# Score matmuls of seven head groups on 64 by 32 array tiles instead of 64 by 64, in a fused attention and two-layer network kernel

## The chip, the cores and the metric

The kernel runs on one core of one Trainium2 chip. The metric is device time of one execution in microseconds (us). The core's engines are TensorE (PE, with its weight loads shown as PEld), VectorE (DVE), ScalarE (ACT), GpSimd (POOL) and SyncE (SP); they run at the same time, each in the order of its own program, and wait for one another through semaphores.

## The reference

Attention with normalised queries and keys, then a two-layer network with a leaky activation. 8 batches, 12 heads, 448 positions, head size 64; the network takes 3584 rows of 768 to 2048 and back.

```python
def rmsnorm(x, g):
    return x / np.sqrt(np.mean(x * x, axis=-1, keepdims=True) + 1e-06) * g
q_n, k_n = rmsnorm(q, g_q), rmsnorm(k, g_k)
scores = np.matmul(q_n, k_n.transpose(0, 1, 3, 2)) / np.sqrt(64)
attn = np.exp(scores - np.max(scores, axis=-1, keepdims=True))
attn = attn / (np.sum(attn, axis=-1, keepdims=True) + 1e-09)
x = np.matmul(attn, v)           # then (batch * position, head * 64)
h = x @ w_in
out = (np.maximum(h, 0.0) + alpha * np.minimum(h, 0.0)) @ w_out
```

## The kernel before

**Tiling.** The twelve heads of a batch are split into two halves g, and a *group* y is two heads of each half: three groups a batch, 24 in all (y = 0 to 23). Each group's queries and keys are squared, summed, scaled and transposed so that the head size lies on the partitions. The 448 keys are cut into J = 7 pieces j of 64. A *score tile* (y, j) holds the scores of one piece of keys against all 448 queries for the four heads: a PSUM tile `sc` of 128 partitions by two banks. Partitions 0 to 63 are half g = 0 and 64 to 127 are g = 1; the two banks are the two heads `par` of each half. There are two such PSUM tiles, used in turn.

**The scores.** `score(y, j)` (L355 to L370) makes one tile. The contraction is over the head size, 64, so a matmul takes 64 rows of the array, and `par` chooses which half of the rows. Its output columns are keys: with m = 64 one matmul gives all 64 keys of a head, four matmuls a tile, each on an array tile of 64 rows by 64 columns (64*64 in the profile). With m = 32 the keys are cut in two (`c`), eight matmuls a tile on array tiles of 64 by 32. Each matmul streams 448 columns and is preceded by its own weight load (the piece of `kT`). L358 chooses m: 64 for y < EARLY, which is 3 * G = 9, else 32. `soft` (L372, ACT at L376) takes the exponential of a whole tile into `expT`.

**Denominators and values.** `den` and `den_pre` sum `expT` over the keys with matrices of ones, `attv` multiplies it with the values. Both use array tiles of 64 by 32 in all groups: `over_keys` (L380, matmuls at L387) and `ones_over` (L411), 56 matmuls a set; PSUM tiles `dn`, `dnb`, `av`, `avb`. Denominators go through ACT (logarithm and exponential, `rden`), and DVE multiplies values by them into `xT`, the input of the network.

**The network.** `up` (matmuls at L501, tiles `hT`, `hTa`, `hTb`) multiplies by `w_in`, ACT and DVE form the activation `gT`, and `down` (L563, `op`, `opa`) and, later, the products of `quad_a`, `quad_b` and `quad_c` (L628, `qx`, `qz`, `qc`) multiply by `w_out`. These matmuls use the whole array, 128 by 128. The transposes of queries and keys (`tps`) do too.

**Order.** The order of all engines' work is written out by hand. The main loop runs over *bursts* n: each has two to four score tiles with their exponentials, in some bursts a set of denominators or values between the tiles, and then a stretch of network work. So TensorE goes from 128 by 128 to the scores' shape, in some bursts to the 64 by 32 of denominators or values and back, and again to 128 by 128. Up to about 34 us there is no network work yet. The first seven groups (y < 7) are transposed on TensorE, the rest by DMA.

**Queues.** Inputs come through SP's queue (and a little ACT's), weights and values through POOL's. The last part of the weights `w_in` and `w_out` lands at 77.5 us, beside the inputs of the next groups.

Of the kernel before, what the change touches and what calls it, by code (L numbers as in the profile page):

```python
# [21 lines left out]
def kernel(  # L22
# [28 lines left out]
    EARLY = 3 * G  # L51
# [303 lines left out]
    def score(y, j):  # L355
        qT, kT = qkT[y, "q"], qkT[y, "k"]
        sc = pss.tile([128, 2, 512], FP32, name="sc", tag="sc")
        m = 64 if y < EARLY else 32  # L358
        for c in range(64 // m):
            for par in range(2):  # L360
                for g in range(2):
                    nc.tensor.matmul(  # L362
                        out=sc[ds(64 * g + m * c, m), par, :S].rearrange(
                            "p (j c) -> p j c", j=J
                        ),
                        lhsT=kT[ds(64 * par, 64), j, g, ts(c, m)],
                        rhs=qT[ds(64 * par, 64), :, g, :],
                        start=True,
                        stop=True,
                    )  # L370
        scs[y, j] = sc
# [409 lines left out]
    m = 0  # L781
    while m < NG * J or steps:
# [21 lines left out]
        while len(bursts[n]) < limit and m < NG * J:  # L804
            y, j = divmod(m, J)
# [244 lines left out]
    for n in range(NB):  # L1050
# [6 lines left out]
        for t in first_tiles:  # L1057
            if t == (0, J - 2):
                spin(1)
            elif t == (1, J - 3):  # L1060
                spin(2, False)
            elif t == (1, J - 2):
                spin(1, False)
            elif t == (0, J - 1):
                turn_one(1, "q")
            elif t == (1, 0):
                turn_one(1, "k")
            elif t == (1, J - 1):
                turn(2)
            score(*t)  # L1070
            if n == den_at[G - 1] - 1 and t == tiles[-1]:
                begin(0)
                begin(1)
            elif lead and t == tiles[0]:
                soft(*t)
                den(dens[n])
                attv(avs[n], 0, True, (log, invert))
            elif lead and t == tiles[1]:
                begin(2)
# [30 lines left out]
        for t in () if lead else tiles[len(first_tiles) : 3]:  # L1110
            score(*t)
            soft(*t)
        if n in avs and len(avs[n]) == 2 and avs[n] != (0, 1):
            attv(avs[n], 1)
        for t in () if lead else tiles[max(len(first_tiles), 3) :]:
            score(*t)
            soft(*t)
# [3 lines left out]
        if n in roots:  # L1121
            y = roots[n]
# [112 lines left out]
```

## Time and profile before

| | us |
|---|---|
| median of 3 runs (413.71 to 420.57) | 417.81 |
| the profiled execution | 417.34 |
| its span, first to last instruction | 415.6 |
| TensorE busy | 398.9 |
| ACT busy | 273.4 |
| DVE busy | 265.8 |
| POOL busy | 255.2 |
| score matmuls 64 by 64, 252 of them, busy | 21.9 |
| score matmuls 64 by 32, 840 of them, busy | 31.8 |

The granted TensorE clock was 0.994 of full speed on average. Matmuls overlap, so that the busy time of a group is the time in which at least one of it ran; a matmul of 448 columns is shown with about 350 ns, while such matmuls follow one another every 189 ns on the whole array. Score tiles of the first nine groups run from 11.4 to 120.6 us, those from group 2 on from 26.7 us.

"issue" as the end of an idle time means that the profile shows nothing that the engine waited for. Instructions are brought to the engines by DMA too; queue 8 of the DMA table is of the kind "instruction".

### The profile page before, as it was taken

What the parts mean: (1) busy time and instruction counts of PE and PEld (TensorE: products, weight loads), DVE (VectorE), ACT (ScalarE), POOL (GpSimd) and SP (SyncE); (2) the same over time, 40 slices, a digit from 0 to 9 for tenths busy, and PEclk for the clock granted to TensorE, in tenths of its full rate; (3) what the DMA queues carried; (4) which work ended last, traced back from release to release, by engine and by line L of the source; (5) the groups of instructions that cost most, each with busy time, mean ns of one, the idle gap of its engine ahead of it and who ended that gap; (6) DMA issues with size and microseconds to landing.
All of it is one profiled execution on the core that took longest, in us unless ns stands there. A gap on an engine that the chain in (4) does not pass through costs nothing. (4 is left out here: it accounts for less than half of the span.)

```text
span 415.6 us, 11768 instructions
## 1 busy us (share of the span) xinstructions
PE 398.9 (96%) x5055; PEld 208.3 (50%) x5055; DVE 265.8 (64%) x421; ACT 273.4 (66%) x390; POOL 255.2 (61%) x180
## 2 busy tenths in 40 slices
PE   6889899999999999989999999999999999999996
PEld 3344345544455445544455445444555445655564
DVE  3876675575556485795788585958577755465322
ACT  4798697778956785666786897884667884135110
POOL 5589695779596974887094857476633507400870
PEclk9899999999999999999999999999999999999999
DMA  8999999976827596829957596279412800320133
GB/s 182 238 234 229 162 210 168 231 193 88 178 36 177 136 125 112 182 64 175 141 81 175 130 211 139 67 167 193 95 41 48 141 4 21 77 58 0 38 95 96
DMA packets 68019, 53.39 MB, mean 128 GB/s; under 512 B 35568, under 2 KB 67456, under 8 KB 67968
## 3 DMA queue, kind: packets, MB, share of 16 engines
q1 hardware_dynamic: 53520, 39.54, 45.5%
q0 software_dynamic: 13472, 11.81, 20.0%
q10 hardware_dynamic: 976, 1.31, 1.3%
q8 instruction: 39, 0.64, 0.7%
q14 instruction: 12, 0.10, 0.1%
HBM read 45.62 MB, written 11.01 MB: 136 GB/s over the span
## 5 line engine op out<-in xcount | busy, mean ns | idle before, releaser
L376 ACT ACTIVATE expT<-sc,expb 128x896 f16<-128x896 f32 x168 | 162.2, 1003 | 45.9 <-PE sc L362 45.7
L501 PE MATMUL hT<-xT,w_in_sb 128*128 128x448 f16 x546 | 113.7, 353 | 2.1 <-issue 1.7
L501 PEld LDWEIGHTS <-w_in_sb 128*128 128x128 f16 x768 | 72.7, 98 | 76.6 <-issue 12.3
L545 DVE TENSOR_TENSOR gT<-hT,gT 128x448 f16<-128x448 f32 x91 | 56.6, 623 | 40.3 <-ACT gT L541 39.2
L210 POOL TENSOR_TENSOR qs<-nat,rr 128x896 f16<-128x896 f32 x36 | 60.5, 1702 | 34.7 <-issue 21.8
L182 POOL TENSOR_TENSOR sq<-nat 128x896 f32<-128x896 f32 x32 | 53.5, 1683 | 41.8 <-DMA nat<-in_q_dram 29.6
L541 ACT ACTIVATE gT<-hT,cols 128x448 f16<-128x448 f32 x90 | 56.9, 633 | 30.0 <-PE hT L501 29.7
L362 PE MATMUL sc<-qT,kT 64*32 64x448 f16 (+1 forms) x1092 | 53.7, 358 | 4.3 <-ACT expT L376 2.0
L628 PEld LDWEIGHTS <-gT 128*128 128x128 f16 x352 | 33.5, 98 | 26.8 <-issue 5.7
L501 PE MATMUL hTa<-xT,w_in_sb 128*128 128x448 f16 x210 | 45.4, 353 | 0.0
L190 DVE TENSOR_REDUCE ss<-sq 128x14 f32<-128x896 f32 (+1 forms) x37 | 38.5, 1052 | 0.9 <-POOL sq L182 0.8
L486 DVE TENSOR_TENSOR xT<-av,rden 64x448 f16<-64x448 f32 (+1 forms) x37 | 27.2, 734 | 14.2 <-PE av L387 8.9
L545 DVE TENSOR_TENSOR gT<-hTa,gT 128x448 f16<-128x448 f32 x35 | 21.8, 623 | 19.5 <-ACT gT L541 19.2
L541 ACT ACTIVATE gT<-hTa,cols 128x448 f16<-128x448 f32 x35 | 22.2, 635 | 18.2 <-PE hTa L501 18.1
L362 PEld LDWEIGHTS <-kT 64*32 64x32 f16 (+1 forms) x1092 | 16.0, 93 | 36.0 <-issue 29.9
L563 PE MATMUL op<-w_out_sb,gT 128*128 128x384 f16 x160 | 27.4, 326 | 0.0
L387 PEld LDWEIGHTS <-vt 64*32 64x32 f16 x1344 | 19.9, 92 | 12.4 <-issue 2.8
L616 POOL TENSOR_TENSOR gs<-gT 128x1024 f16<-128x1024 f16 x3 | 6.4, 2125 | 30.4 <-DVE gT L545 28.1
L563 PEld LDWEIGHTS <-gT 128*128 128x128 f16 x192 | 18.0, 98 | 13.4 <-issue 2.3
L387 PE MATMUL av<-expT,vt 64*32 64x448 f16 x896 | 24.3, 350 | 0.3 <-DVE osb L676 0.3
L624 POOL TENSOR_TENSOR gT<-gT 128x1024 f16<-128x1024 f16 x11 | 23.4, 2128 | 0.0
L628 PE MATMUL qx<-w_out_sb,gT 128*128 128x384 f16 x120 | 20.8, 326 | 1.2 <-DVE rden L430 1.2
(149 smaller groups left out, 494.0 us busy)
## 6 DMA issues: line engine op xcount, KB each, us to landing
out_dram<-osb SPq DMA_DIRECT2D x107, 96.0 KB, 3.0
nat<-in_q_dram SPq DMA_DIRECT2D x40, 224.0 KB, 4.2
nat<-in_k_dram SPq DMA_DIRECT2D x40, 224.0 KB, 5.1
vt<-in_v_dram POOLq DMA_DIRECT2D x16, 336.0 KB, 8.0
w_in_sb<-in_moe_w_in_dram POOLq DMA_DIRECT2D x12, 256.0 KB, 7.8
w_out_sb<-in_moe_w_out_dram POOLq DMA_DIRECT2D x4, 768.0 KB, 9.7
arena<-in_q_dram SPq DMA_DIRECT2D x6, 224.0 KB, 7.4
arena<-in_k_dram SPq DMA_DIRECT2D x6, 224.0 KB, 6.8
```

The source lines that it names most:

```text
L182: nc.gpsimd.tensor_mul(out=sqf[:, c], in0=src[:, c], in1=src[:, c])
L190: nc.vector.tensor_reduce(out=o[:, c], in_=sqs[y, nm][:, c], axis=AXIS_X, op=ALU.add)
L210: eng.tensor_mul(out=t.rearrange("p j h d -> p h j d"), in0=nat[y, nm], in1=rr_t[y][:, "qk".index(nm)].unsqueeze(3).broadcast_to((128, 2, ...
L362: nc.tensor.matmul(out=sc[ds(64 * g + m * c, m), par, :S].rearrange("p (j c) -> p j c", j=J), lhsT=kT[ds(64 * par, 64), j, g, ts(c, m)], r ...
L376: nc.scalar.activation(out=expT[y][:, j], in_=scs[y, j][:, :, :S], func=AF.Exp, scale=QK_SCALE, bias=expb[:, 0:1],)
L387: nc.tensor.matmul(out=accs[g][ds(32 * n, 32), :S], lhsT=weights(g, y, par, c, j), rhs=expT[y][ds(64 * g, 64), j, par, :], start=(j == 0), ...
L486: nc.vector.tensor_mul(out=x, in0=av, in1=r)
L501: nc.tensor.matmul(out=hT[:, :S], lhsT=w_in_sb[:, g * G + i, ts(ft, 128)], rhs=xT[b][:, g, i, :], start=(i == 0 and g == 0), stop=(i == G ...
L541: nc.scalar.activation(out=g, in_=hT[:, :S], func=AF.Copy, scale=alpha_sb[:, ft : ft + 1])
L545: nc.vector.tensor_max(out=g, in0=hT[:, :S], in1=g)
L563: nc.tensor.matmul(out=op[:, :OH], lhsT=gT[:, ft, ts(tile % J, 128)], rhs=w_out_sb[:, ft, ts(oh, OH)], start=(ft == 0), stop=(ft == NF - 1),)
L628: nc.tensor.matmul(out=bank[:, c], lhsT=g[:, ft], rhs=v[:, ft, c], start=(first and ft == 0), stop=(ft == HF - 1), skip_group_check=True,)
```

## The change

One line of `score`: the bound below which m is 64 goes from EARLY (9) to 2. Groups 0 and 1 keep array tiles of 64 by 64; groups 2 to 8, the third to the ninth, get 64 by 32, as groups 9 to 23 have. A tile of theirs is then eight matmuls with eight weight loads instead of four with four; outputs, inputs and everything else stay.

```diff
     def score(y, j):
         qT, kT = qkT[y, "q"], qkT[y, "k"]
         sc = pss.tile([128, 2, 512], FP32, name="sc", tag="sc")
-        m = 64 if y < EARLY else 32
+        m = 64 if y < 2 else 32
         for c in range(64 // m):
             for par in range(2):
                 for g in range(2):
```

## The prediction

> **What bounds the kernel now.** I read the page first: busy shares, the slices, then the chain that ended last.
>
> ```profile
> PE 398.9 (96%) x5055; PEld 208.3 (50%) x5055; DVE 265.8 (64%) x421; ACT 273.4 (66%) x390; POOL 255.2 (61%) x180
> ...
> PE 29%; DVE 1%; ACT 0%; issue 0%; DVEq 0%
> ...
> q8 instruction: 39, 0.64, 0.7%
> ```
>
> TensorE is busy 96% of the span, and the chain back from the end hardly leaves it. So from about 43 us on, TensorE time saved or lost arrives at the end nearly one for one. The third row matters later: TensorE's 10,110 instructions are far the most of any engine, and 39 instruction packets of 16.4 KB are 256 instructions each if they are TensorE's (39 x 256 = 9,984).
>
> Next, TensorE's timeline (start, length, instruction, count) in a burst of 64x64 scores (first line group) and in a late burst that is already 64x32:
>
> ```profile
> 68.67 0.57 PE L362 MATMUL sc<-qT,kT 64*64 64x448 f16 x8
> 69.17 1.52 PE L387 MATMUL dn<-expT,ones 64*32 64x448 f16 x56
> 70.62 0.38 PE L362 MATMUL sc<-qT,kT 64*64 64x448 f16 x4
> 70.93 2.77 PE L563 MATMUL op<-w_out_sb,gT 128*128 128x384 f16 x16
> ```
> ```profile
> 157.21 0.57 PE L362 MATMUL sc<-qT,kT 64*32 64x448 f16 x16
> 157.60 1.51 PE L387 MATMUL dn<-expT,ones 64*32 64x448 f16 x56
> 158.92 0.37 PE L362 MATMUL sc<-qT,kT 64*32 64x448 f16 x8
> 159.23 2.77 PE L563 MATMUL op<-w_out_sb,gT 128*128 128x384 f16 x16
> ```
>
> The same work, three score tiles and one set of denominators, takes 70.93 - 68.67 = 2.26 us with two changes of array shape inside it and 159.23 - 157.21 = 2.02 us with none: 0.12 us a change. Twice the matmuls cost nothing themselves: eight 64x32 ones run together as four 64x64 ones do (two tiles alone between 128x128 work take 89.87 to 90.38 = 0.51 us as 64x64, and 0.50 us late in the kernel as 64x32).
>
> Last, the one long idle time of TensorE between 30 and 170 us, and the windows around it (window, length, TensorE busy and count, weight loads, DVE, ACT, POOL, granted clock, DMA share, GB/s):
>
> ```profile
> 39.92 1.69 PE L501 MATMUL hTb<-xT,w_in_sb 128*128 128x448 f16 x8
> 43.33 0.92 PE L501 MATMUL hT<-xT,w_in_sb 128*128 128x448 f16 x4 [1.72 <-issue]
> ```
> ```profile
> 36.52:43.32 6.80, 5.09 (x128) 2.56 (x128) 1.47 (x2) 3.77 (x4) 6.55 (x7) 1.00 1.15 219
> 68.60:92.50 23.90, 23.75 (x417) 11.97 (x417) 13.53 (x20) 17.77 (x24) 14.98 (x10) 1.00 0.99 211
> 92.50:122.00 29.50, 29.32 (x342) 14.38 (x340) 16.01 (x25) 23.35 (x34) 24.30 (x17) 1.00 0.57 98
> ```
>
> The values' last input, xT, is written by DVE until 41.45, yet TensorE starts at 43.33, released by nothing that the profile shows. At 36.28 a score tile is also torn: its first matmul starts at 36.28, the other three from 36.52. Between the two restarts lie 128 matmuls and 128 weight loads, exactly 256 instructions: one packet of the instruction queue. The packets fit (the DMA view, narrowed until one instruction packet fills it): one runs from 33.76 to 34.94 and TensorE goes on at 36.52; the next from 40.87 to 41.80, and it goes on at 43.33, some 1.55 us behind the packet each time. So TensorE here runs out of instructions, and one block is on its way while one is worked off. From entering a block (36.52) to having the next (43.33) took 6.80 us while the DMA engines were full (share 1.15). At 70 to 77 us the next close call: entry between 69.6 and 70.6, packet until 75.44, the block's first instruction at 76.69, with the queue just empty: 6.1 to 7.1 us, and nothing lost. Above 110 us, with the share at 0.57, packets start 0.2 to 3 us after the entry, and I count no such stall.
>
> **The change part by part.** It touches the scores of groups 2 to 8, 49 tiles.
>
> *Removed: changes of shape.* Only bursts with denominators or values have them. By the timeline after 60 us, from the first score to the next other work, against the late twin: 68.67 burst 0.24 (two changes); 73.64 to 77.67, two sets of values, 4.03 against 3.53 (165.83 to 169.36) = 0.50; 80.37, whose denominators wait 0.15 us for DVE anyway, only the way back, 0.10; 84.90 0.24; 110.47, which waits 0.18 us, 0.12; 118.28 to 121.88, 3.60 against 3.23 = 0.37. Sum 1.57 us, all on the path. The changes before 42 us are not counted: what is gained there ends in the wait for the instruction packet. The bursts with scores alone: 0.
>
> *Added: instructions.* 49 tiles x 4 matmuls, each with its weight load, = 392, one and a half blocks. Their run time is nothing (above); their fetch is the unknown of this change, bounded by 0 (packets early enough, as above 110 us) and 8.0 us a block (from 28.5, the earliest entry before the 36.52 restart). I take 6.8, the one row where both ends are seen, in the same stretch. Each block now ends earlier in the program, by 8 instructions for each changed tile before it.
>
> *The first stretch, by that price.* The block that ended at 36.52 has seven changed tiles ahead and ends 56 instructions earlier, in the transposes of group 3 (the eleventh of fourteen, at 33.4 on the old clock). Its predecessor is entered some 0.4 us sooner (16 instructions, and two changes of shape saved), so the packet serves at 36.1. TensorE stands from 33.4 to 36.1. Then: three transposes 0.15, score tile (2,5), tile (2,6) and the eight hT matmuls to 38.4, tile (3,0) to 38.7. The denominators of group 2 need (2,6) through ACT, two exponentials of 0.9 us a step behind (2,5)'s scores at 36.9: 38.8. They start at 39.0 instead of 36.84. The following block (64 instructions earlier, two thirds through the values at 38.17) is wanted at 41.1 and comes at 36.1 + 6.8 = 42.9. Then the rest of the values 0.45, tile (3,1) 0.6, eight hTb 1.5: the hT matmuls of 43.33 start at 45.5. Meanwhile xT is ready at 44.7. Loss 2.2 us, in place of the old stall and not on top of it. With packets as prompt as later this would be 0; at 8.0 us a block 3.6.
>
> *The second stretch.* Between 53 and 73 us a block lasts 8 us and more: no wait. The block that is entered at the scores of 73.64 ends with the tile at 77.35, less 0.61 us of saved changes, 76.7. The sequencer reaches it early: the 16 matmuls ahead are 32 instructions, and earlier packets (81.6 to 85.64, 92.7 to 96.28) start 4 us behind the instruction 64 places before the entry, which is here 70.6. With 6.1 to 7.1 us behind that: 76.7 to 77.7. I take 0.4 us; if the sequencer isn't ahead, it is 73.4 + 6.8 = 80.2, a loss of 3.5. The next block, 7.2 us long, is covered. Above 92 us the ends only move; the shortest stretch from the place 64 ahead of an entry to the block's end is 6.2 us where it was 5.9: 0.
>
> *Sum:* -1.57 + 2.2 + 0.4 = +1.0 us. The profiled execution took 417.34 us (span 415.6, 1.7 around it), so 418.4; the median of the runs shown is 0.5 above it, so **418.9 us**.
>
> [...]
>
> **The rivals.**
> - *The packets come in time; only changes of shape remain.* For it: above 110 us none is late, and DMA traffic is not the same in every execution. Against: shares of 1.15 and 0.99 in the two stretches, two late packets in this trace. It decides from a fetch below about 5 us. Median 417.8 - 1.6 = 416.2, still within 2%.
> - *The lateness adds up.* At 8.0 us a block the first stretch costs 3.6; a sequencer not ahead at 73.4 gives a block at 81.4, 4.7, and 0.8 at the next, which is 7.2 long. The standing engine may lose its clock: after a 3.4 us window with 1.07 us busy (7.9 to 11.3) the granted clock was 0.50 for the next one; the window 31.8 to 35.2 would keep about 1.5 busy, and half a clock there costs up to 1.7. Sum 3.6 + 4.7 + 0.8 + 1.7 - 1.6 = +9.2: 427. Against: every term at its worst.
> - *Little of anything:* half of the early loss is taken up by ACT's and DVE's slack: -1.57 + 1.1 + 0.2, about 417.5. This is inside the forecast's own range.
>
> **How the numbers follow.** Forecast (with the last rival) 0.52, its own range 416.5 to 421.5; packets in time 0.23; adding up 0.25, of which some 0.20 pass the bound. 2% (8.4 us) is about what a measurement of this kernel can tell from no change; its three runs spread from 413.7 to 420.6. Faster by more would need five times the saving that I find: 0.04. Slower 0.20, within 0.76. Range for 8 in 10: from 414.9 (the first rival, less a little spread) to 426 (most of the second).
>
> **What would show it.** Right: the scores at 68.67 to the op matmuls take 2.0 us; a TensorE idle time released by "issue" among the transposes near 33.4 and one inside the values of group 2, 256 instructions apart, each 1.5 us behind an instruction packet; the first hT after xT at about 45.5; hT and op matmuls of the same lengths as before. Wrong: no such idle times (first rival), several near 77 to 86 us or a granted clock of 0.5 near 35 us (second), or a difference that starts after 122 us, where I put nothing.

## The result and the profile after

The changed kernel took 419.06 us (median of 13 runs, 417.48 to 421.14), the kernel before 417.26 us over 13 runs. The ratio is 1.0077, 95% interval 1.0051 to 1.0103: 2.1 to 4.3 us slower, 3.2 in the middle. The ratio goes by the fast runs of each kernel and is no quotient of the two medians, which lie 1.8 us apart. A second set of six runs, on the same chip as two other kernels, gave 1.0112 (1.0066 to 1.0158). The profiled execution took 418.89 us, its span is 417.1.

Page of the changed kernel, the rows that were shown of the one before:

```profile
PE 397.3 (95%) x5251; PEld 209.6 (50%) x5251; DVE 267.7 (64%) x421; ACT 273.3 (66%) x390; POOL 256.1 (61%) x180
...
PE 29%; DVE 1%; ACT 0%; issue 0%; DVEq 0%
...
q8 instruction: 41, 0.67, 0.7%
```

196 matmuls and 196 weight loads more, two instruction packets more, and TensorE is busy for 1.6 us less while the span is 1.5 us longer. The time went into standing.

The timeline of TensorE in the changed kernel (start, length, instruction, count, idle time ahead of it) shows where:

```profile
31.59 0.79 PE L335 MATMUL tps<-ident,arena 128*128 128x128 f16 x11
34.19 0.34 PE L335 MATMUL tps<-ident,arena 128*128 128x128 f16 x3 [1.81 <-issue]
...
38.11 1.12 PE L387 MATMUL av<-expT,vt 64*32 64x448 f16 x37
42.03 0.74 PE L387 MATMUL av<-expT,vt 64*32 64x448 f16 x19 [2.79 <-issue]
...
44.42 0.92 PE L501 MATMUL hT<-xT,w_in_sb 128*128 128x448 f16 x4
```

The row of fourteen transposes is torn after eleven, the values of group 2 after 37 of 56, and nothing in the profile releases TensorE from either pause. The old pause ahead of the hT matmuls is gone: they now follow the hTb matmuls at once. The windows view of the changed kernel (window, length, TensorE busy and count, weight loads, DVE, ACT, POOL, granted clock, DMA share, GB/s) counts what lies between the two restarts:

```profile
34.19:42.02 7.83, 5.04 (x128) 2.41 (x128) 2.67 (x3) 4.78 (x5) 7.61 (x9) 1.00 1.16 230
```

Again 128 matmuls and 128 loads: one block of 256 instructions, whose successor took 7.8 us to come.

Setting the same matmuls of both profiles side by side, counted in the program, gives the course of the difference (start in the changed kernel less start in the one before, us):

| matmul | before at | difference |
|---|---|---|
| denominators at 27.54 | 27.54 | -1.41 |
| first hT after xT | 43.33 | +1.09 |
| denominators of group 3 and 4 | 69.17 | +0.97 |
| avb | 75.90 | +0.50 |
| opa, behind the tile at 77.35 | 77.67 | +0.99 |
| opa | 122.19 | +0.24 |
| hT | 137.12 | +1.75 |
| qx | 179.50 | +1.17 |
| from 284 to the end | | +1.55 |

Of the -1.41, 1.28 us stand before the first changed instruction (the score at 26.72 of the kernel before); the rest is its first change of shape. In the profile of before the granted clock was 0.50 from 11.3 to 14.7 us, in that of after it was 1.00 up to the last microseconds. So this pair of profiles hides some 1.3 us of the loss: 1.5 + 1.3 = 2.8 us, within the 2.1 to 4.3 of the ratio.

Second stretch, TensorE's timeline of the changed kernel:

```profile
69.76 0.57 PE L362 MATMUL sc<-qT,kT 64*32 64x448 f16 x16
70.14 1.51 PE L387 MATMUL dn<-expT,ones 64*32 64x448 f16 x56
71.47 0.37 PE L362 MATMUL sc<-qT,kT 64*32 64x448 f16 x8
71.78 2.77 PE L563 MATMUL op<-w_out_sb,gT 128*128 128x384 f16 x16
...
77.72 0.35 PE L362 MATMUL sc<-qT,kT 64*32 64x448 f16 x1
78.34 0.38 PE L362 MATMUL sc<-qT,kT 64*32 64x448 f16 x7 [0.27 <-issue]
```

The burst that took 2.26 us takes 71.78 - 69.76 = 2.02 us, as its late twin does. The tile that stood at 77.35 is torn after its first matmul: the third block that comes late.

### The profile page after: what moved, and what is told of

The parts are those of the page before. It is cut to its first block, busy times and chain, and to the rows that moved or that the text cites. A ratio compares the mean times of both kernels' runs of the same rounds, so it can differ in the third digit from the quotient of the medians.

```text
span 417.1 us, 12160 instructions
## 1 busy us (share of the span) xinstructions
PE 397.3 (95%) x5251; PEld 209.6 (50%) x5251; DVE 267.7 (64%) x421; ACT 273.3 (66%) x390; POOL 256.1 (61%) x180
## 5 line engine op out<-in xcount | busy, mean ns | idle before, releaser
L210 POOL TENSOR_TENSOR qs<-nat,rr 128x896 f16<-128x896 f32 x36 | 61.5, 1727 | 42.2 <-issue 23.7
L387 PEld LDWEIGHTS <-vt 64*32 64x32 f16 x1344 | 21.0, 93 | 14.4 <-issue 4.8
```

Of the source, the lines that this page charges most:

```text
L210: eng.tensor_mul(out=t.rearrange("p j h d -> p h j d"), in0=nat[y, nm], in1=rr_t[y][:, "qk".index(nm)].unsqueeze(3).broadcast_to((128, 2, ...
L387: nc.tensor.matmul(out=accs[g][ds(32 * n, 32), :S], lhsT=weights(g, y, par, c, j), rhs=expT[y][ds(64 * g, 64), j, par, :], start=(j == 0), ...
```

## The experiments

The theory, worked out from the kernel before (256 instructions between the restarts at 36.52 and 43.33, the packet of the second block from 40.87 to 41.80, DMA share 1.15): TensorE's instructions come in blocks of 256, one block ahead; where small matmuls are dense and the DMA engines full, a block is worked off before the next is there. Rivals: the smaller array tiles cost by themselves; the cost sits after 85 us, in GpSimd and the loads behind it; the pause ahead of hT is a wait for data; a fetch takes its time whatever else goes on.

**The two halves of the change.** Groups 5 to 8 alone, then groups 2 to 4 alone:

```diff
-        m = 64 if y < EARLY else 32
+        m = 64 if y < 5 else 32
```
```diff
-        m = 64 if y < EARLY else 32
+        m = 64 if y < 2 or 5 <= y < EARLY else 32
```

> 64 by 32 for groups 5 to 8 alone (m = 64 if y < 5), so nothing changes before 64 us. Theory (TensorE runs out of instruction blocks where small matmuls are dense and the DMA engines full): the stretch 26 to 46 us is as in the kernel before, with its one idle time of up to 1.9 us ahead of the hT matmuls; the bursts from 68 to 122 us win back 1.3 us of changes of shape; a block that ends among the denominators near 81 us may come late by up to 1.4 us. Net -1.3 to +0.1 us, ratio 0.997 to 1.000. Rival (the late half of the change costs by itself, through GpSimd and the loads that fall behind it after 85 us): slower by 1 us or more, ratio 1.003 or above, with the GpSimd squares near 87 us waiting over 1.5 us.

> 64 by 32 for groups 2 to 4 alone (and from 9 on as before). Theory (instruction blocks): two idle times of TensorE without a releaser, at the eleventh transpose of group 3 (about 2 us) and two thirds through the values of group 2 (about 3 us), 256 instructions apart, in place of the one ahead of the hT matmuls; +2 to +3 us at 46 us and at the end, ratio 1.005 to 1.007, since these groups' changes of shape are won only where TensorE waits anyway. Rival (the cost sits late, the early idle time is absorbed): ratio within 0.998 to 1.002.

Groups 2 to 4 alone: 1.0054 (1.0024 to 1.0084). TensorE's timeline:

```profile
35.15 0.34 PE L335 MATMUL tps<-ident,arena 128*128 128x128 f16 x3 [2.75 <-issue]
...
42.71 0.74 PE L387 MATMUL av<-expT,vt 64*32 64x448 f16 x19 [2.52 <-issue]
```

The two pauses are at the eleventh transpose and in the values of group 2: place and ratio as the theory had them. The profiled execution was the longest of its set (422.61 us, the median is 419.03): behind the second pause its granted clock was 0.50 from 43.67 to 47.09 us, which the theory had not foreseen.

Groups 5 to 8 alone: 1.0051 (1.0028 to 1.0074). The ratio is the rival's, not the theory's. Its mechanism is not seen: the GpSimd squares near 85 us waited 2.24 and 0.35 us for their inputs, against 1.73 and 0.38 in the kernel before. What costs is on TensorE (timeline, then windows of TensorE with busy time, count, granted clock, DMA share and GB/s, of groups 5 to 8 alone):

```profile
78.52 0.76 PE L411 MATMUL dn<-expT,ones 64*32 64x224 f16 x45
81.23 0.37 PE L411 MATMUL dn<-expT,ones 64*32 64x224 f16 x11 [1.95 <-issue]
81.34 0.44 PE L362 MATMUL sc<-qT,kT 64*32 64x448 f16 x8
81.72 4.45 PE L563 MATMUL op<-w_out_sb,gT 128*128 128x384 f16 x16
```
```profile
78.81:82.22 3.41, 1.46 (x60) 1.00 1.24 208
82.22:85.63 3.41, 3.41 (x12) 0.50 1.09 221
```

The block that was expected to end among the denominators near 81 us does, and it comes 2 us late (expected: up to 1.4). Behind the pause the clock is halved for 3.4 us, so that sixteen matmuls take 4.45 us instead of 2.77. The pause and the clock together, 3.6 us, are what this half loses in this profile; up to there it was 0.6 us ahead by the changes of shape. So the theory's place was right and its price too low: the pause alone passes the 1.4 us that I allowed, and I had left the clock out.

**Instructions without the shape.** Old shapes everywhere; in groups 2 to 4 each tile gets four more matmuls of 64 columns into columns of its banks that nobody reads:

```diff
+        if 2 <= y < 5:
+            for par in range(2):
+                for g in range(2):
+                    nc.tensor.matmul(
+                        out=sc[ds(64 * g, 64), par, S:512],
+                        lhsT=kT[ds(64 * par, 64), j, g, :],
+                        rhs=qT[ds(64 * par, 64), 0, g, :],
+                        start=True,
+                        stop=True,
+                    )
```

> All shapes as in the kernel before, but each score tile of groups 2 to 4 gets four more 64 by 64 matmuls of 64 columns into the unused columns of its banks: the instruction count of the run before (8 more a tile), none of its shapes. Theory (instruction blocks): the same two idle times at the same two places as with 64 by 32 in groups 2 to 4, of 1.5 to 3 us each, and +2 to +3 us, plus the run time of the added matmuls, at most 0.1 us for each of 21 tiles. Rival (the shape itself, its weight loads or the exponentials' order cost the time): no idle time at these places, the old one ahead of hT stays, and only the added run time of 0.5 to 2 us is seen.

1.0066 (1.0035 to 1.0096). TensorE's timeline of this kernel:

```profile
33.57 0.79 PE L335 MATMUL tps<-ident,arena 128*128 128x128 f16 x11
36.77 0.34 PE L335 MATMUL tps<-ident,arena 128*128 128x128 f16 x3 [2.41 <-issue]
...
40.91 1.12 PE L397 MATMUL av<-expT,vt 64*32 64x448 f16 x37
42.69 0.75 PE L397 MATMUL av<-expT,vt 64*32 64x448 f16 x19 [0.66 <-issue]
```

The same two tears, after the same eleventh transpose and the same 37th matmul, without one score on a 64 by 32 tile. The second is shorter than expected (0.66 us against 1.5 or more), since the added matmuls and a quicker packet (5.9 us from restart to restart) close the gap. So the count of instructions sets the place of the pauses, and the shape isn't needed for them. The size of the loss is less clear: from the transposes at 25.58 of the kernel before to the hT matmuls at 43.33 this profile lost 1.0 us, with the added matmuls' own time in it, the first profile of the change 2.4.

**The ends of the blocks moved.** Old shapes, and 200 more instructions at the start, where TensorE waits for inputs anyway (in the kernel before, its first work behind the warming matmuls starts at 8.70 us, after 0.75 us released by the DMA of `in_g_k_dram`): 8 of the 17 warming matmuls give way to 108 tiny ones.

```diff
-    spin(17, False)
+    spin(9, False)
+    fill = psf.tile([128, 512], FP32, name="fill", tag="mm")
+    for n in range(108):
+        c = n % 4
+        nc.tensor.matmul(
+            out=fill[ds(32 * c, 32), :16], lhsT=ones[ds(64 * (c % 2), 64)],
+            rhs=idle[ds(64 * (c % 2), 64), :16], start=True, stop=True,
+        )
```

> The kernel before with its scores untouched; of the 17 warming matmuls at the start 8 are replaced by 108 tiny ones (16 columns, 64 by 32), so that 200 more instructions lie ahead of all blocks and every block ends 56 instructions later in the program than before (200 = 256 - 56). Theory (instruction blocks): the idle time of 1.7 us ahead of the hT matmuls and the torn score tile near 36 us go, since each block of the stretch 30 to 46 us is now wanted 6.8 us or more after the one ahead of it; -1.0 to -1.8 us, ratio 0.996 to 0.998. Rival (that idle time is a wait for xT, weights or a bank that the profile doesn't show): it stays as it is, 1.7 us, and the time is unchanged or longer by the added matmuls.

> Once more the old shapes with 200 more instructions ahead (0.9953 to 1.0018 so far). Theory: 0.996 to 0.999; the idle time ahead of hT, which is 0.2 to 1.7 us in the profiles seen with the blocks in their old places, is gone each time. Rival: 1.000 or above.

First 0.9985 (0.9953 to 1.0018), in the second set 0.9975 (0.9950 to 1.0000). The pause ahead of hT is gone in both profiles. TensorE's timeline in the first:

```profile
40.09 1.69 PE L501 MATMUL hTb<-xT,w_in_sb 128*128 128x448 f16 x8
41.66 0.92 PE L501 MATMUL hT<-xT,w_in_sb 128*128 128x448 f16 x4
```

xT, weights and banks are the same, so it was no wait for those. Counted in the program, the hT matmuls came 2.07 us sooner relative to the transposes at 32.86. The time gained is less than that, and the interval of each set still reaches 1: the old pause is not there in full in every execution (it was 0.22 us in the profile of groups 5 to 8 alone, which is the same program up to 62 us). What the padding itself costs at the start can't be told apart from scatter: at the transposes at 25.58 the profiles with it stand -1.42 to +0.98 us from the kernel before, those without it -1.28 to +0.87.

**The whole change with other block ends** (96 tiny matmuls, 176 more instructions):

> The whole change (groups 2 to 8), with 96 tiny matmuls ahead (176 more instructions), so that the blocks end elsewhere. Theory (instruction blocks): the two idle times at the eleventh transpose and in the values of group 2 go; one of 0.4 to 1.4 us stays near 42 us, ahead of the hT matmuls, and one of 1 to 2 us comes near 85 us, perhaps with half a clock behind it; -1 to +1.5 us against the kernel before, better than the change by 1 to 3 us. Rival (the shape or the count of matmuls costs at its own place, wherever the blocks end): the idle times stay among the transposes and values, ratio 1.006 to 1.009.

1.0023 (0.9982 to 1.0064), against 1.0077 and 1.0112 of the change itself. TensorE's timeline:

```profile
31.38 0.56 PE L387 MATMUL avb<-expT,vt 64*32 64x448 f16 x13 [0.78 <-issue]
...
37.58 1.50 PE L387 MATMUL dn<-expT,ones 64*32 64x448 f16 x51 [0.41 <-issue]
...
43.52 0.38 PE L362 MATMUL sc<-qT,kT 64*32 64x448 f16 x8 [0.40 <-PE hT L501]
```

The long pauses at the old places are gone; three short ones came, 256 instructions apart. The profile puts the third down to an hT matmul, but it too ends a block, 1.35 us behind an instruction packet. Their places were expected for one of three only, and none came near 85 us.

**Less DMA traffic.** The whole change, with three quarters of `w_in` issued later:

```diff
-    after(5, load_w_in, 1)
+    after(8, load_w_in, 1)
-    after(7, load_w_in, 2)
-    after(8, load_w_in, 3)
+    after(9, load_w_in, 2)
+    after(10, load_w_in, 3)
```

> The whole change, but the second, third and fourth quarter of w_in are issued after bursts 8, 9 and 10 instead of 5, 7 and 8, so that the DMA engines have less to do between 33 and 41 us. Read from the trace up to 41 us only; later the network waits for w_in, several us. Theory (a block comes late because its packet waits behind other DMA traffic): the instruction packet that came 5.0 us behind the entry of its block (39.2 us against 34.2) starts 1 to 2.5 us behind it, and the idle time in the values of group 2 (2.8 us) shrinks to 0.5 us or less. Rival (fetching a block takes this long whatever else the DMA engines do): 3.5 to 5 us, idle time unchanged.

Windows of this kernel between its two restarts, and its second restart:

```profile
34.08:39.44 5.36, 5.04 (x128) 2.41 (x128) 2.67 (x3) 4.07 (x5) 5.36 (x6) 1.00 0.57 131
```
```profile
39.45 0.74 PE L387 MATMUL av<-expT,vt 64*32 64x448 f16 x19 [0.33 <-issue]
```

With the DMA share at 0.57 instead of 1.16 the same 256 instructions were followed by the next block after 5.4 us instead of 7.8, and the pause shrank from 2.79 to 0.33 us. The packet started 2.8 us behind the entry of its block instead of 5.0; I had expected 1 to 2.5. The rival's 3.5 to 5 us are not seen here, and this fits a packet that waits behind other DMA traffic. But it is one run, and it doesn't show that cause. With the DMA engines as full as ever, the packet between the same two blocks started 2.4 us behind the entry in the kernel with added instructions (36.77 to 39.17, share 1.11 to the next restart) and 2.7 us with groups 5 to 8 alone (35.83 to 38.53, share 1.12). And in this run the share was still 0.94 up to the packet's start and 0.15 from there to the restart: the packet may have come when the traffic ahead of it ended, or as early as in those two kernels without that. What makes a packet late stays open. The kernel as a whole took 420.46 us in one run, with the network waiting 1.6 us for `w_in`.

**A version from both findings.** Groups 5 to 8 with 180 more instructions ahead, and groups 6 to 8 with 202 (the second in two sets of runs):

> 64 by 32 for groups 5 to 8, with the ends of the instruction blocks moved: 9 of the 17 warming matmuls and 98 tiny ones at the start, 180 more instructions ahead. Theory (instruction blocks): no idle time ahead of hT near 43 us, none of 2 us among the denominators near 81 us (at most 0.5 us near 75), no half clock behind it, and the 1.3 us of changes of shape are won: -2.5 to -3.3 us against the kernel before, ratio 0.992 to 0.995. Rival (the late 64 by 32 scores cost by themselves): no better than the shift alone with old shapes, ratio 0.998 or above.

> 64 by 32 for groups 6 to 8 only, 109 tiny matmuls ahead (202 more instructions). Theory: no late block at all up to 92 us; -1.7 us for the idle time ahead of hT, -0.9 us for the changes of shape from 77 us on: ratio 0.993 to 0.995. Rival (late 64 by 32 scores cost by themselves): 0.998 or above.

> Once more 64 by 32 for groups 6 to 8 with 202 more instructions ahead, to narrow its interval (0.9942 to 1.0006 so far). Theory: 0.995 to 0.998, below 1 in both sets of runs. Rival (nothing is won in most executions, since the old idle time ahead of hT is often short): 0.999 to 1.001.

Groups 5 to 8: 1.0002 (0.9970 to 1.0034), short of the theory's 0.995; a block still comes 0.97 us late at 74.4 us in its profile (expected: at most 0.5), and no 2 us pause at 81. Groups 6 to 8: 0.9974 (0.9942 to 1.0006) and 0.9979 (0.9950 to 1.0007), whose timelines have no idle time without a releaser between 26 and 122 us, and 0.9 us won from 76 to 122 us in the first profile. Both intervals just include 1. The middle of both lies about 1 us below the kernel before, clearly below the change, and no lower than that of the shifted blocks alone.

**The change again**, beside those:

> The change itself, on the same chip as these two: 1.005 to 1.010 as measured at first, with the idle times at the eleventh transpose of group 3 and in the values of group 2, whose lengths differ from execution to execution (1.8 and 2.8 us in the first profile); 0.007 to 0.011 above the two others.

1.0112 (1.0066 to 1.0158). In this profile the first pause was 2.56 us, and the clock followed (windows of TensorE: busy time, count, granted clock, DMA share, GB/s):

```profile
32.00:35.40 3.40, 1.48 (x35) 1.00 1.18 222
35.42:42.24 6.82, 5.84 (x59) 0.50 1.15 228
```

At half clock TensorE reached the values so late (43.02 us, against 38.11 in the first profile) that their block was there and all 56 ran in one piece; from the denominators at 27.54 to the hT matmuls it lost 3.0 us all the same.

## Why the prediction came out as it did

The time, 418.9 us forecast and 419.06 measured, agrees by luck more closely than its parts. Forecast was +1.0 us on the kernel before; the ratio says +3.2 (2.1 to 4.3), so the direction and the places held and the loss was forecast too small. Up to the opa matmuls at 122.19, counted from the transposes at 25.58, the two profiles of the change lost 1.5 and 2.4 us.

- *Changes of shape, 1.57 us.* Held per change: 0.25 us at the burst of 68.67, 0.25 at 84.90, 0.13 at 110.47, 0.36 at 118.28 in the first profile, against 0.24, 0.24, 0.12 and 0.37. The 0.10 of the way back at 80.37 did not come: the op matmuls behind it kept their lag of 0.99. In 73.64 to 77.67 the late block hides the end.
- *Twice the matmuls cost nothing themselves.* Held: the burst takes 2.02 us as its late twin does, and TensorE is busy for 397.3 us, where it was 398.9.
- *The first stretch, 2.2 us.* Both places were right, to the transpose and to two thirds of the values, and the old pause was replaced and not kept. From -1.41 to +1.09 the first profile lost 2.5 us, the second 3.0. The single lengths were off: the first block came sooner (1.8 us of standing instead of 2.7; 2.75 with groups 2 to 4 alone, 2.56 in the second profile), the second took 7.8 us instead of 6.8 (2.8 instead of 1.8). One price could not fit: between these two blocks 5.3 to 7.8 us passed in the profiles with the DMA share at 1.11 to 1.16. The 256 instructions that I read in the kernel before hold, with one correction: they are 127 matmuls, 128 weight loads and one semaphore instruction; the window's 128th matmul had begun ahead of it.
- *The second stretch, 0.4 us.* 0.49 us in the first profile, at the tile of 77.35 as said; 0.95 in the second.
- *Above 92 us, 0.* No idle time of 0.2 us or more without a releaser is there in either kernel, though the packets start over a wider stretch than the 0.2 to 3 us given above 110 us: in the kernel before from 2.9 us ahead of the entry of a block (393.54 against 396.41) to 5.1 us behind it (154.56 against 149.51). From 122 us to the end the first profile lost another 1.3 us: +1.5 at 137 us, where DVE's copies stood behind a reduction that waited 2.04 us for its square, and the square 3.08 us for its input, and -1.1 at 179. The second profile of the change gained 0.35 us over the same part, the two of the shifted blocks 0.4 and 0.3. I read it as scatter between executions; no run isolates it, and the cause stays open.
- *The step that was mis-sized* is the price of a late block. I took the old pause of 1.7 us ahead of hT as always there, to be replaced, where it is 0.22 us in the profile of groups 5 to 8 alone; I took 6.8 us a block where up to 7.8 were seen; and I put the halved clock into the rival alone, where the second profile of the change has it (0.50 from 35.41 to 42.24), and so have the profiles of both halves. The terms that I named for "the lateness adds up" were right in kind: they came in part, and not all at their worst. The first rival, packets in time, fell: of two profiles of the change none was without the pauses, and nine of the thirteen profiles of all kernels have at least one idle time of 0.2 us or more at the end of a block.

## What to carry to other kernels

A matmul that is split in two can cost no array time and still cost an instruction fetch (here 1.6 us less TensorE time and 3.2 us more in all): count TensorE's instructions per microsecond where the DMA engines are full, not only its busy time. A pause that the profile gives no releaser, torn into the middle of a group of matmuls, with exactly 256 instructions to the next one, was a late block here: in the kernel before, the change and the change with other block ends an instruction packet ended 1.3 to 1.6 us ahead of the restart. Padding where the engine waits anyway moved it (200 more instructions: no pause ahead of hT in two profiles, where it had been 1.72 us), and with half the score matmuls in groups 2 to 4 there was, in place of the pauses of 1.81 and 2.79 us, one of 1.72 us (the kernel before) or 0.22 us (groups 5 to 8 alone). That less DMA traffic brings a block sooner is likely and not shown. Keep uniform shapes for stretches in which the DMA engines are half idle: behind 92 us, where the share in the kernel before is 0.57, none of the thirteen profiles has an idle time of 0.2 us or more without a releaser.

## What the hardware showed that was not expected

Pauses of 1.95 us (groups 5 to 8 alone), 2.52 us (groups 2 to 4 alone) and 2.56 us (the change again) were followed by a halved clock. Windows of 3.4 us, as long as the stretch of half clock in the kernel before (11.3 to 14.7 us), with 1.46 us (groups 5 to 8 alone) and 1.48 us (the change again) of TensorE busy were followed by a clock of 0.50; in the first profile of the change one with 1.78 us, from 40.39 to 43.81, was not. TensorE's busy time in the window doesn't decide it alone: with groups 5 to 8 alone, a later window with the same 1.46 us (283.60 to 287.01) kept the full clock, and an early one with 2.23 us (17.36 to 20.77) was followed by 0.50, where in the kernel before one with 2.24 us (18.14 to 21.55) was not. The two windows of 1.46 and 1.48 us that were followed by half clock were idle for little more than half of their length.

From the end of an instruction packet to the first instruction of its block passed 1.59 and 1.52 us at the two restarts of the kernel before, and 1.54, 1.38 and 1.32 us at the three pauses of the first profile of the change.
